# v of batch 0's first four heads in one load and product, seven dummies behind ident for twelve, w_in's last load split, batch 2's sums called one quarter ahead

## The chip, the cores and the metric

The kernel runs on one core of one Trainium2 chip. The metric is the device time of one execution in microseconds (us). Four runs of the kernel before gave 502.73, 502.10, 504.18 and 502.46 us, a median of 502.6. One more execution was profiled; its own time was 503.14 us, of which 501.4 us lie between the first and the last instruction (the span). All times of day below are counted from the start of that span.

## The reference, cut to what matters

Attention in which keys and values are first projected along the sequence (1024 rows to 64), then a feed-forward layer with a hard-swish-like gate:

```python
k_proj = np.einsum('ks,bhsd->bhkd', E, k)          # 8 batches, 8 heads, 1024 x 64 -> 64 x 64
v_proj = np.einsum('ks,bhsd->bhkd', F, v)
attn = softmax(q @ k_proj^T / sqrt(64))            # 1024 x 64 for each head
x = (attn @ v_proj), heads side by side            # 8192 tokens x 512
h = x @ w_in                                       # 512 -> 2048
out = (h * clip(h + 3, 0, 6) / 6) @ w_out          # 2048 -> 512
```

Inputs and output are float32; the kernel multiplies in bfloat16 and sums in float32.

## The kernel before, in words

The work goes batch by batch, and each batch in two blocks of 512 tokens (`t`). For a block, sixteen groups `first_group` (`fo`) make the hidden layer `g`, each of eight matmuls with the stationary half as wide as the array (L169, two of them side by side on the array), a Relu on ACT (L513) and a multiply on DVE (L514). Four groups `second_group` then multiply a block's `g` with `w_out`, each in four quarters of eight matmuls, copy the result out of PSUM and store it by SP (L549). The attention of a later batch is placed by hand between these groups: a dictionary `plan` says, for slot `n` (0 to 7 in a batch) and quarter, which piece of it is recorded there (L654 to L668). The scheduling is manual: every engine executes its instructions in the order in which the Python code records them, and the framework adds only the waits.

For batches 2 to 7 the softmax's sums are made by DVE: `add_up` (L270) reduces the exponentials of each pair of heads, `spread_sums` (L279 to L284) turns, adds and inverts them, and SP writes the result to DRAM (L287) and reads it back broadcast as `rec` (L293). The products of attention and v are multiplied with `rec` on DVE (L262). For batch 2, inside the pass over batch 1 (`b == 1`), the last of these calls, `end_of_sums`, stands at slot 5, quarter 2.

Batch 0 has no earlier work to hide behind, and has a class of its own, `First`. The opening:

- SP and ACT load E and F (L78, L79); DVE sets `ones`; TensorE runs twelve dummy matmuls on `ones` (L89). They compute nothing that is used.
- POOL issues the loads of batch 0, in an order written by hand: k and half of q by pairs of heads (L106, L102), with the identity matrix `ident` made by POOL between the first and the second pair; then four pairs of v; then w_in in eight pieces of columns (L125), the other half of q, w_out (L133) and the inputs of batch 1 (L120). A load waits for the landing of the load eight places before it.
- E and F are cast, transposed on TensorE with `ident` (L145), and copied to `e_t` and `f_t`.
- `first_block` goes over four pairs of heads: `keys` (L375, copied by DVE at L378), `queries` (transposes, L405, L409), `scores` (L418) with exponentials on ACT (L445), `keys_transposed` (L384, L386) and `sums` (L425), whose logarithm and exponential on ACT (L450, L451) give the reciprocal. A few single dummies stand in between.
- Then come, in this order: `vals(0)` (the projection of v for heads 0 and 1: eight matmuls at L391 into PSUM and a copy at L394), `sums(2)`, `vals(1)`, `products(0)` (attention times v on PE at L425, times the reciprocal on DVE at L454, into `xT`), `sums(3)`, `vals(2)`, `products(1)`, a dummy, `products(2)`, `vals(3)` with its copy on ACT, the first two matmuls of the hidden layer, and `products(3)`. After that the hidden layer of block 0 runs on.

Of the kernel before, what the change touches and what calls it, by code (L numbers as in the profile page):

```python
# [15 lines left out]
def kernel(  # L16
# [11 lines left out]
    nc = tc.nc  # L28
# [5 lines left out]
    P = 128  # L34
    SO = S // P
    KO = d_model // P
# [29 lines left out]
    def pmm():  # L66
        return ps_mm.tile([P, TOK], f32, tag="mm", name="mm")

    def pat():
        return ps_at.tile([P, TOK], f32, tag="at", name="at")  # L70


    def g_tile():
        return gpool.tile([P, FO, TOK], bf16, tag="g", name="g")
# [6 lines left out]
    ones = consts.tile([P, TOK], bf16, name="ones")  # L81
    nc.vector.memset(ones, 1.0)  # L82
    ident = consts.tile([P, P], bf16, name="ident")


    def busy(n):
        ps = pmm()
        for _ in range(n):
            nc.tensor.matmul(ps, ones[:, :P], ones, start=True, stop=True)  # L89

    busy(12)

    def raw_tile(name):
        return kqv_pool.tile([P, H, SO, D], bf16, tag=name, name=name)


    kqv = {0: {n: raw_tile(n) for n in ("k", "q", "v")}}
# [3 lines left out]
    def load_q0(t, hs):  # L101
        nc.gpsimd.dma_start(out=q0[:, t, hs], in_=kqv_dram["q"][0][:, hs, t * SB:(t + 1) * SB, :])  # L102

    def load_pair(n, j):
        hs = slice(2 * j, 2 * j + 2)
        nc.gpsimd.dma_start(out=kqv[0][n][:, hs], in_=kqv_dram[n][0][:, hs])  # L106

    for j in range(KO):
        load_pair("k", j)
        load_q0(0, slice(2 * j, 2 * j + 2))  # L110
        if j == 0:
            make_identity(nc, ident)
    for j in range(KO):
        load_pair("v", j)

    def load_kqv(b, order="qkv"):
        kqv[b] = {}
# [6 lines left out]
    def load_w_in(lo, n):  # L124
        nc.gpsimd.dma_start(out=w_in_sb[:, :, lo:lo + n], in_=w_in_v[:, :, lo:lo + n])  # L125

    for lo, n in ((0, 128), (128, 128), (256, 256), (512, 256), (768, 256),
                  (1024, 256), (1280, 256), (1536, 512)):
        load_w_in(lo, n)
    load_q0(1, slice(0, H))  # L130
    for i in range(SB):
# [6 lines left out]
    f_t = consts.tile([P, SO, 2, KP], bf16, name="f_t")  # L138
# [9 lines left out]
    for a in range(2):  # L148
        nc.scalar.copy(f_t[:, :, a, :], ef_pv[:, 1])
    ef_t = [e_t, f_t[:, :, 0, :]]  # L150
    busy(2)

    def q_transposed(b):
# [33 lines left out]
    class Attention:  # L187
# [66 lines left out]
        def sums(self, j, *allocs):  # L254
            return self.quads(lambda r, h: ones[r:r + KP, :D], j, allocs)
# [108 lines left out]
    class First:  # L364
# [20 lines left out]
                                    self.kp[:, 2 * j + a].rearrange("p a d -> p (a d)"), ident[:KP, :KP])  # L385
            nc.vector.tensor_copy(self.kT[:, 2 * j:2 * j + 2, :].rearrange("p h m -> p (h m)"), ps)  # L386

        def vals(self, j, copy):
            ps = pat()[:, :P]
            for so in range(SO):  # L390
                nc.tensor.matmul(ps, f_t[:, so].rearrange("p a m -> p (a m)"),  # L391
                                 kqv[0]["v"][:, 2 * j:2 * j + 2, so, :],
                                 start=(so == 0), stop=(so == SO - 1))
            copy(self.vp[:, 2 * j:2 * j + 2, :].rearrange("p h d -> p (h d)"), ps)  # L394

        def queries(self, t, js):

# [39 lines left out]
        def first_block(self, meanwhile):  # L437
            recs = {}

            def scores(j):  # L440
                aT = att.tile([P, 2, HT], bf16, tag="aT0", name="aT0", bufs=KO)
                tiles = [pmm() for _ in range(2)]
                self.scores(0, j, tiles, 0)
                for r in range(2):
                    nc.scalar.activation(aT[:, r], tiles[r][:, :HT], AF.Exp, scale=scale)  # L445
                self.aT[0, j] = aT

            def sums(j):
                recs[j] = opool.tile([P, TOK], f32, tag="o_sb", name="o_sb")
                nc.scalar.activation(recs[j], self.sums(0, j, pmm), AF.Ln)  # L450
                nc.scalar.activation(recs[j], recs[j], AF.Exp, scale=-1.0)  # L451

            def products(j):
                nc.vector.tensor_mul(self.xT[:, j, 0, :], self.values(0, j, pat), recs[j])  # L454

            for j in range(KO):
                self.keys(j)
                if j > 1:
                    sums(j - 2)
                self.queries(0, (j,))  # L460
                if j > 0:
                    scores(j - 1)
                else:
                    busy(1)
                self.keys_transposed(j)
                if j < 2:
                    busy(1)
            scores(KO - 1)
            self.vals(0, nc.vector.tensor_copy)
            sums(KO - 2)  # L470
            self.vals(1, nc.vector.tensor_copy)
            products(0)
            sums(KO - 1)
            self.vals(2, nc.vector.tensor_copy)
            products(1)
            busy(1)
            products(2)
            self.vals(3, nc.scalar.copy)
            meanwhile()
            products(3)  # L480
# [35 lines left out]
    def first_group(xT, t, g, fo):  # L516
        h_ps = pmm()
        h_part(h_ps, xT, t, fo, range(KO))
        h_out(h_ps, g, fo)
# [31 lines left out]
    def whole(gen):  # L551
        for _ in gen:
            pass

    def x_tile():
        return xpool.tile([P, KO, NB, TOK], bf16, tag="xT", name="xT")
# [27 lines left out]
    def meanwhile():  # L584
        early.append(TwoGroups(xT, 0, g[0]))
        early[0].part(0, (0,))
# [13 lines left out]
    second = Attention(1)  # L600
    second.xT = x_next

    def pop():
        if later:
            later.pop(0)()
# [28 lines left out]
    second = Attention(2)  # L634
    for b in range(1, B):
        if b + 1 < B:
            x_next = second.xT = x_tile()
        third = Attention(b + 2) if b + 2 < B else None


        plan = {}
        two, more = ((pmm, pmm), (pat, pat)), (pat, pat)

        def end_of_sums():
            second.add_up(3)
            second.spread_sums()

        if b == 1:
            def fourth_scores():
                while later:  # L650
                    pop()
                second.some_scores((3,), two)

            plan = {(4, 1): fourth_scores, (4, 2): lambda: second.add_up(0, 1, 2), (5, 2): end_of_sums,  # L654
                    (6, 1): second.first_values, (6, 4): second.first_products,
                    (7, 1): lambda: second.some_values((2, 3), two)}
        elif b + 1 < B:
            plan = {(5, 2): lambda: second.some_values((0, 1), two),
                    (6, 2): lambda: second.some_values((2, 3), two, third)}
            if third:  # L660
                plan[4 if b == 2 else 3, 2] = third.projected
            if b == 2:
                plan.update({(0, 2): second.projected, (1, 4): second.all_scores,
                             (2, 2): lambda: second.add_up(0, 1, 2), (3, 2): end_of_sums})
            else:
                plan.update({(0, 1): lambda: second.some_scores((1, 2, 3), (*two, more)),
                             (0, 2): lambda: second.add_up(0), (1, 2): lambda: second.add_up(1, 2),
                             (2, 2): end_of_sums})  # L668


        slots = (0, 3, 11, 15) if b == 1 else (3, 7, 11, 15)
        for t in range(NB):
            g = g_tile()
            for fo in range(FO):
                if b < 3 and t == 0 and fo < 2:

                    if fo == 0:
                        TwoGroups(xT, t, g).parts((0, 1, 2), (3,))
                else:
                    first_group(xT, t, g, fo)  # L680
                pop()
                if b == 1 and t == 0 and fo == 1:
                    second.projected()
                elif b == 1 and t == 0 and fo == 14:
                    second.some_scores((2, 0, 1), (*two, more), later.append)
                if not behind or fo not in slots:
                    continue
                n = t * SB + slots.index(fo)

                rows = second_group(*behind[0], n % SB,  # L690
                                    nc.vector.tensor_copy if second and plan.get((n, SB)) == second.all_scores else None)
                for quarter in range(1, SB + 1):
                    next(rows) if quarter < SB else whole(rows)
                    if (n, quarter) in plan:
                        plan[n, quarter]()
            behind = [(b, t, g)]
        if b == 1:
            later.append(lambda: qT_dma.update({3: q_transposed(3)}))
        second, xT = third, x_next
# [32 lines left out]
```

## Time and profile before

| | us |
|---|---|
| median of four runs (502.10 to 504.18) | 502.6 |
| the profiled execution, its own time | 503.14 |
| its span, first to last instruction | 501.4 |
| PE busy | 494.6 (99% of the span) |
| DVE busy | 285.4 (57%) |
| ACT busy | 239.6 (48%) |
| POOL busy | 38.7 (8%) |
| start of the steady stream of matmuls at L169 | 20.77 |

In the lines of the profile, PE is the matmul, PEld the weight load that overlaps it, DVE VectorE, ACT ScalarE, POOL GpSimd and SP SyncE; L12 is line 12 of the kernel; `out<-in` are the program's own names of tiles. A line of the timeline gives the start, the length, the engine, the line, the operation, how often it ran in a row (x8), and in brackets how long the engine sat idle before it and what ended that. The chain of waits is followed back from the last instruction: each piece is a start, a length and what ran. Busy shares are averages over the whole span, and a matmul's end is modelled, so PE's 99% says that it always had something in hand, not that it ran at its peak.

Loads of the opening, by the landing events of the trace (issue on POOL, landing):

| load | issue | landing |
|---|---|---|
| k, pair 0 | 1.24 | 6.23 |
| k, pair 3 | 6.16 | 12.61 |
| q half, pair 3 | 6.87 | 13.29 |
| v, pair 0 | 7.58 | 14.56 |
| v, pair 1 | 8.29 | 15.84 |
| v, pair 2 | 9.00 | 17.12 |
| v, pair 3 | 9.71 | 18.42 |
| w_in, columns 0 to 127 | 10.94 | 20.06 |
| w_in, last 512 columns | 18.70 | 29.83 |
| q, other half | 20.34 | 32.59 |

### The profile page before, as it was taken

To read this page: it belongs to the slowest core of one execution; us is meant where nothing else is said; L and a number is where in the kernel's file an instruction comes from. 1 tells how busy PE (TensorE), PEld (TensorE's weight loads), DVE (VectorE), ACT (ScalarE), POOL (GpSimd) and SP (SyncE) were. 2 spreads that over 40 slices of the span, in tenths; PEclk is the share of its full clock that TensorE was granted. 3 is DMA by queue.
4 is the path that set the end of the run, shared out by engine and by line. 5 is a ranking of instruction groups with operands and counts; after the bars stand their busy time and mean duration, and the time that the engine had idled before them with its cause. 6 is when DMAs were issued, how large, how long until landed. Compare 5 with 4: busy or idle time off the path is not lost.

```text
span 501.4 us, 11177 instructions
## 1 busy us (share of the span) xinstructions
PE 494.6 (99%) x4802; PEld 256.5 (51%) x4802; DVE 285.4 (57%) x438; ACT 239.6 (48%) x414; POOL 38.7 (8%) x58
## 2 busy tenths in 40 slices
PE   8999999999999999999999999999999999999997
PEld 4554554555555445555555555555455555555554
DVE  3572736886659665666638655674755656334420
ACT  3657566665354345533564344643456344343431
POOL 8620020200020020002000020000000000000000
PEclk9999999999999999999999999999999999999999
DMA  9999999898759699549960799309511261101112
GB/s 167 198 204 207 188 172 234 149 211 177 181 94 221 140 217 212 115 107 228 204 129 22 172 192 221 83 24 221 126 43 44 59 176 44 43 22 43 44 43 84
DMA packets 83618, 68.43 MB, mean 136 GB/s; under 512 B 38256, under 2 KB 69232, under 8 KB 83568
## 3 DMA queue, kind: packets, MB, share of 16 engines
q0 software_dynamic: 32480, 29.36, 37.5%
q1 hardware_dynamic: 50864, 38.02, 30.9%
q8 instruction: 37, 0.61, 0.5%
q10 hardware_dynamic: 224, 0.33, 0.3%
q14 instruction: 13, 0.11, 0.1%
HBM read 71.83 MB, written 16.97 MB: 177 GB/s over the span
## 4 chain that ended last, share of the span: by engine, by line
PE 94%; DMA 5%; POOL 1%; issue 0%; SPq 0%; ACT 0%; ACTq 0%; POOLq 0%
PE mm L169 87%; PE at L169 2%; DMA w_in_sb<-in_moe_w_in_dram 2%; DMA qT<-q 2%; DMA k<-in_k_dram 1%; PE mm L250 1%; PE at L229 1%; PE at L250 1%; PE mm L229 1%; PE at L425 0%; POOL q L102 0%; POOL k L106 0%; PE at L405 0%; PE at L418 0%; POOL ident masks.py:199 0%
## 5 line engine op out<-in xcount | busy, mean ns | idle before, releaser
L514 DVE SCALAR_TENSOR_TENSOR g<-r,mm 128x512 bf16<-128x512 f32 x256 | 174.3, 687 | 144.3 <-ACT r L513 143.6
L169 PE MATMUL mm<-w_out_sb,g 128*64 128x512 bf16 (+2 forms) x2080 | 235.6, 376 | 0.0
L169 PE MATMUL mm<-xT,w_in_sb 128*64 128x512 bf16 x2048 | 231.1, 379 | 0.2 <-DMA w_in_sb<-in_moe_w_in_dram 0.2
L513 ACT ACTIVATE r<-mm 128x512 f32<-128x512 f32 x256 | 152.7, 598 | 74.4 <-PE mm L169 73.4
L169 PEld LDWEIGHTS <-w_in_sb 128*64 128x64 bf16 x2048 | 115.8, 110 | 104.9 <-issue 0.6
L169 PEld LDWEIGHTS <-g 128*64 128x64 bf16 x2080 | 115.0, 110 | 106.3 <-issue 7.1
L548 ACT COPY o_sb<-mm 128x512 f32<-128x512 f32 x58 | 34.0, 586 | 149.9 <-PE mm L169 149.5
L270 DVE TRANSPOSE_TENSOR_REDUCE parts<-aT 128x32 f32<-128x1024 bf16 x24 | 28.8, 1226 | 0.0
L262 DVE TENSOR_TENSOR xT<-at,rec 128x512 bf16<-128x512 f32 x32 | 20.5, 683 | 8.7 <-ACT rec L181 5.8
L238 ACT ACTIVATE aT<-at 128x512 bf16<-128x512 f32 x38 | 20.7, 620 | 8.7 <-PE at L229 8.7
L262 DVE TENSOR_TENSOR xT<-mm,rec 128x512 bf16<-128x512 f32 x24 | 15.5, 686 | 7.3 <-PE mm L250 7.2
L219 POOL COPY mark<-qT 1x1 bf16<-1x1 bf16 x5 | 0.9, 177 | 203.0 <-DMA qT<-q 203.0
L205 DVE CAST kp<-at 64x512 bf16<-64x512 f32 x14 | 9.0, 678 | 11.3 <-PE at L169 11.2
L169 PE MATMUL at<-k,e_t 128*64 128x512 bf16 x56 | 13.2, 379 | 0.0
L169 PE MATMUL at<-v,f_t 128*64 128x512 bf16 x56 | 13.2, 379 | 0.0
L238 ACT ACTIVATE aT<-mm 128x512 bf16<-128x512 f32 x18 | 9.7, 603 | 7.1 <-PE mm L229 7.1
L208 DVE CAST vp<-at 64x512 bf16<-64x512 f32 x14 | 9.7, 694 | 0.4
L538 DVE COPY o_sb<-mm 128x384 f32<-128x384 f32 x1 | 0.6, 558 | 15.2 <-PE mm L169 15.2
L169 PEld LDWEIGHTS <-e_t 128*64 128x64 bf16 x56 | 6.2, 110 | 5.7
L89 PE MATMUL mm<-ones 128*128 128x512 bf16 x18 | 7.4, 549 | 1.5 <-DVE ones L82 1.5
L229 PEld LDWEIGHTS <-kT 64*64 64x64 bf16 x224 | 5.6, 106 | 5.6 <-issue 4.7
L229 PE MATMUL at<-qT,kT 64*64 64x256 bf16 x152 | 6.2, 269 | 0.9 <-DMA qT<-q 0.9
(68 smaller groups left out, 148.2 us busy)
## 6 DMA issues: line engine op xcount, KB each, us to landing
out_dram<-o_sb SPq DMA_DIRECT2D x63, 256.0 KB, 4.4
rec<-turned_rows SPq DMA_DIRECT2D x48, 256.0 KB, 6.3
k<-in_k_dram POOLq DMA_DIRECT2D x7, 1024.0 KB, 10.6
v<-in_v_dram POOLq DMA_DIRECT2D x7, 1024.0 KB, 16.4
q<-in_q_dram POOLq DMA_DIRECT2D x7, 1024.0 KB, 20.8
w_out_sb<-in_moe_w_out_dram POOLq DMA_DIRECT2D x4, 512.0 KB, 16.1
w_in_sb<-in_moe_w_in_dram POOLq DMA_DIRECT2D x5, 256.0 KB, 9.8
k<-in_k_dram POOLq DMA_DIRECT2D x4, 256.0 KB, 5.6
```

Of the source, the lines that this page charges most:

```text
L89: nc.tensor.matmul(ps, ones[:, :P], ones, start=True, stop=True)
L169: nc.tensor.matmul(ps[lo:lo + width], stationary[:, lo:lo + width], moving, **flags)
L205: nc.vector.tensor_copy(self.kp[:, :, a, :], self.ps[:KP].rearrange("p (h d) -> p h d", d=D))
L208: nc.vector.tensor_copy(self.vp[a * KP:(a + 1) * KP], self.ps[KP:].rearrange("p (h d) -> p h d", d=D))
L229: nc.tensor.matmul(tiles[r][t * KP:(t + 1) * KP, a * HT:(a + 1) * HT], self.kT[r * D:(r + 1) * D, 2 * j + a, :], qT[r * D:(r + 1) * D, j, ...
L238: when(lambda r=r: nc.scalar.activation(aT[:, :, r, :], tiles[r].rearrange("p (a n) -> p a n", a=2), AF.Exp, scale=scale))
L250: nc.tensor.matmul(tiles[t][c:c + D], stationary(r, 2 * j + a), self.weights(j, a)[r:r + KP], start=True, stop=True)
L262: when(lambda t=t: nc.vector.tensor_mul(self.xT[:, j, t, :], av[t], rec[:, t]))
L270: nc.vector.tensor_reduce(out=self.parts[:, j], op=ALU.add, axis=mybir.AxisListType.X, apply_transpose=True, in_=self.aT[j].rearrange("p a ...
L513: nc.scalar.activation(r, h_ps, AF.Relu, bias=0.5, scale=1.0 / 6.0)
L514: nc.vector.scalar_tensor_tensor(g[:, fo, :], r, 1.0, h_ps, op0=ALU.min, op1=ALU.mult)
L548: (copy or nc.scalar.copy)(o_sb, o_ps)
```

## The change

Five edits:

- the dummies at the start are seven instead of twelve, are recorded after `ident` has been made, and use `ident` instead of `ones` as the stationary (as do all other dummies);
- v of heads 0 to 3 of batch 0 comes in one load instead of two;
- the projection of these four heads is one product of eight matmuls with 256 columns instead of two with 128, with one copy, and `sums(2)` is recorded between its fourth and fifth matmul; `sums(3)` comes next, and `products(0)` and `products(1)` come ahead of `vals(2)`;
- the last 512 columns of w_in come in two loads instead of one;
- `end_of_sums` of batch 2 stands at quarter 1 of slot 5 instead of quarter 2.

```diff
-            nc.tensor.matmul(ps, ones[:, :P], ones, start=True, stop=True)
-
-    busy(12)
+            nc.tensor.matmul(ps, ident, ones, start=True, stop=True)
...
-    def load_pair(n, j):
-        hs = slice(2 * j, 2 * j + 2)
+    def load_pairs(n, j, more=1):
+        hs = slice(2 * j, 2 * (j + more))
         nc.gpsimd.dma_start(out=kqv[0][n][:, hs], in_=kqv_dram[n][0][:, hs])
...
         if j == 0:
             make_identity(nc, ident)
-    for j in range(KO):
-        load_pair("v", j)
+            busy(7)
+    load_pairs("v", 0, 2)
+    for j in range(2, KO):
+        load_pairs("v", j)
...
-                  (1024, 256), (1280, 256), (1536, 512)):
+                  (1024, 256), (1280, 256), (1536, 256), (1792, 256)):
...
-        def vals(self, j, copy):
-            ps = pat()[:, :P]
+        def vals(self, j, copy, more=1, halfway=lambda: None):
+            hs = slice(2 * j, 2 * (j + more))
+            ps = pat()[:, :more * P]
             for so in range(SO):
-                nc.tensor.matmul(ps, f_t[:, so].rearrange("p a m -> p (a m)"),
-                                 kqv[0]["v"][:, 2 * j:2 * j + 2, so, :],
+                nc.tensor.matmul(ps, f_t[:, so].rearrange("p a m -> p (a m)"), kqv[0]["v"][:, hs, so, :],
                                  start=(so == 0), stop=(so == SO - 1))
-            copy(self.vp[:, 2 * j:2 * j + 2, :].rearrange("p h d -> p (h d)"), ps)
+                if so == SO // 2 - 1:
+                    halfway()
+            copy(self.vp[:, hs, :].rearrange("p h d -> p (h d)"), ps)
...
             scores(KO - 1)
-            self.vals(0, nc.vector.tensor_copy)
-            sums(KO - 2)
-            self.vals(1, nc.vector.tensor_copy)
-            products(0)
+            self.vals(0, nc.vector.tensor_copy, 2, lambda: sums(KO - 2))
             sums(KO - 1)
+            products(0)
+            products(1)
             self.vals(2, nc.vector.tensor_copy)
-            products(1)
             busy(1)
             products(2)
...
-            plan = {(4, 1): fourth_scores, (4, 2): lambda: second.add_up(0, 1, 2), (5, 2): end_of_sums,
+            plan = {(4, 1): fourth_scores, (4, 2): lambda: second.add_up(0, 1, 2), (5, 1): end_of_sums,
```

More of the change, by code (lines that the diff above doesn't have):

```diff
@@ L102, in load_q0 @@
         nc.gpsimd.dma_start(out=q0[:, t, hs], in_=kqv_dram["q"][0][:, hs, t * SB:(t + 1) * SB, :])
-    def load_pair(n, j):
-        hs = slice(2 * j, 2 * j + 2)
+    def load_pairs(n, j, more=1):
+        hs = slice(2 * j, 2 * (j + more))
         nc.gpsimd.dma_start(out=kqv[0][n][:, hs], in_=kqv_dram[n][0][:, hs])
     for j in range(KO):
-        load_pair("k", j)
+        load_pairs("k", j)
         load_q0(0, slice(2 * j, 2 * j + 2))
@@ L468, in first_block @@
             scores(KO - 1)
-            self.vals(0, nc.vector.tensor_copy)
-            sums(KO - 2)
-            self.vals(1, nc.vector.tensor_copy)
+            self.vals(0, nc.vector.tensor_copy, 2, lambda: sums(KO - 2))
+            sums(KO - 1)
             products(0)
-            sums(KO - 1)
+            products(1)
             self.vals(2, nc.vector.tensor_copy)
-            products(1)
             busy(1)
```

## The prediction

> **What bounds the kernel now.** I read the page's busy times first, then the chain of work that ended last in order of time, then the timeline of the first 22 us.
>
> ```profile
> PE 494.6 (99%) x4802; PEld 256.5 (51%) x4802; DVE 285.4 (57%) x438; ACT 239.6 (48%) x414; POOL 38.7 (8%) x58
> ```
>
> TensorE is busy for 494.6 of 501.4 us, so a change pays only where the matmul stream starts earlier or loses a gap. The chain shows two such places:
>
> ```profile
> 10.94 9.12 DMA w_in_sb<-in_moe_w_in_dram
> 20.11 0.41 PE mm L169 x2
> 20.51 0.33 PE at L425 x2
> 20.84 12.85 PE mm L169 x118
> ...
> 176.03 8.01 DMA qT<-q
> 184.09 0.41 PE at L229 x8
> ```
>
> The steady stream begins at 20.77 (20.84 in the chain's rounding); from there one piece of PE follows another, but for one wait of about 1 us at 184.09, for the transposed q of batch 4. The change touches the time ahead of 20.77 and, by its words, batch 2 around 109. In the timeline of the opening the reader is to see how tightly PE, DVE and ACT hand work to each other:
>
> ```profile
> 1.46 5.30 PE L89 MATMUL mm<-ones 128*128 128x512 bf16 x12 [1.46 <-DVE ones L82]
> 5.58 0.62 ACT L141 CAST g<-g 128x512 bf16<-128x512 f32 x1 [2.95 <-DMA g<-in_E_dram]
> 6.55 0.90 PE L145 MATMUL at<-ident,g 128*128 128x128 bf16 x8
> 7.29 0.59 PE L89 MATMUL mm<-ones 128*128 128x512 bf16 x2
> ...
> 16.51 0.40 PE L425 MATMUL mm<-aT,ones 64*64 64x512 bf16 x2
> ...
> 17.50 0.29 DVE L394 CAST vp<-at 128x128 bf16<-128x128 f32 x1 [0.66 <-PE at L391]
> ...
> 17.91 0.69 DVE L454 TENSOR_TENSOR xT<-at,o_sb 128x512 bf16<-128x512 f32 x1
> ...
> 18.52 0.28 DVE L394 CAST vp<-at 128x128 bf16<-128x128 f32 x1
> ...
> 18.95 0.40 PE L425 MATMUL at<-aT,vp 64*64 64x512 bf16 x2
> ...
> 20.44 0.40 PE L425 MATMUL at<-aT,vp 64*64 64x512 bf16 x2
> ...
> 20.77 1.49 PE L169 MATMUL mm<-xT,w_in_sb 128*64 128x512 bf16 x12
> ```
>
> **Batch 2's sums: nothing.** The call moves from the second to the first quarter of one slot. Between those quarters only matmuls are recorded, on PE's queue; the call itself records only on DVE (L270, L279 to L284) and SP (L287, L293). No other DVE, ACT or SP instruction stands between the two places, so every queue keeps its order. In the trace the last reduce of batch 2 starts at 109.50, when the multiply of g before it (108.90 + 0.69) ends: it waits for DVE, not for a quarter. Cost and gain 0. The products at 121.84 still wait 1.9 us for their sums, and PE shows no gap there.
>
> **The loads: about nothing.** The load queue is full: in the stretches from 7 to 21 us the 16 DMA engines show a share of 1.27 to 1.49 (packets overlap) and move 183 to 203 GB/s. Loads land in order: the landing events put the four v pairs at 14.56, 15.84, 17.12 and 18.42, the first w_in piece at 20.06. Merging two v loads saves one issue on POOL (0.75 us) and moves no byte, so I put the double load's landing at 15.84, where the second pair lands today, and the first w_in piece at 20.06. Each load waits for the one eight places earlier, so all later ones shift by one place until the split of the last w_in restores the count; q's second half is issued about 0.7 us later (now 20.34) behind a queue that is still full. It lands at 32.59 today and is needed at 33.70. The split itself hides: the last w_in lands at 29.83, its first use is about 12 groups of 0.86 us behind 20.8. If that cover were gone, each later us of landing would cost a us. Bounds: -0.1 to +0.3; I take 0.
>
> **One product for v's first four heads: +0.93 us.** Today PE runs product, sums, product, then the first attention product (17.40), whose v projection was copied long before. After, I follow the new order with durations of the rows.
> - The product of v starts at 15.89 as now: the scores before it end then, and 15.84 + 0.05 is the landing. A pair of 512-column matmuls takes 0.218 (12.85 us for 118 in the chain), so a 256-column one is spaced 0.11, and four end their issue at 16.34. The sums wait for the exponentials until 16.51, as now. The other four run from 16.84 to 17.18, and the last result stands at 17.45.
> - DVE copies 256 columns. 128 columns take 0.29, 64x512 take 0.68 (L205), so about 0.42: 17.49 to 17.91. PE does the fourth sums at 17.38 and then has nothing: the first attention product needs this copy and starts at 17.97 (+0.06, as after e_t: 7.91 to 7.97). That is +0.57 against 17.40.
> - The second follows at 18.19, the third v product at 18.52 to 18.92 (now 17.74).
> - DVE takes its queue in order, and the copy of this third product now stands behind two multiplies of xT instead of one: 18.45, then 19.11 (spacing 0.66 as at 18.80), then the copy 19.72 to 20.00 (now 18.52 to 18.80). PE's third attention product starts at 20.06; now 18.95. This is the term that decides: +1.11.
> - The fourth v product 20.39 to 20.79, ACT's copy of it 21.05 to 21.31, the first piece of the hidden layer (now held until 20.11 by w_in, which has landed by then) 20.94, the fourth attention product 21.37; now 20.44. So +0.93: 0.18 of the delay comes back because that w_in wait vanishes.
> - The stream begins at 21.70 instead of 20.77. The fourth multiply ends at 22.6, and the matmuls that need it come at 21.70 + 5 x 0.216 = 22.78, so no further wait.
>
> What is queued behind PE's two new waits is everything, since PE's order is fixed.
>
> **Seven dummies for twelve: -0.07 to +0.9, I take +0.17.** Ident is ready at 3.35, so the dummies start near 3.45 instead of 1.46; the first is spaced 0.40, the others 0.43 (weight loads at 4.85, 5.27, 5.70), and the transposes start at 6.41 instead of 6.55; the casts they also need end at 6.20. These 0.14 us run through the keys' chain, but the double load of v (15.84) and PE's four wide matmuls give back half: -0.07. Against it stands TensorE's rate. In the trace dummies are spaced 0.43 up to 6.1 and 0.21 at 7.29 (0.59 for two, less 0.38 for one), while the granted clock reads 1.00 throughout. If full rate comes at the same time, 7.1 to 7.3, the gain of 0.07 stands. If it comes the same time after the first dummy (7.29 - 1.46 = 5.83, hence 9.28), two dummies and the first keys run at half rate: transposes to 7.27, dummies to 8.12, keys at 8.15 instead of 7.97, eight matmuls at 0.107 instead of 0.056, thus +0.6; should it last over the next queries and dummies too, +0.9. The first is nearer to the row, the others keep a share.
>
> The Trainium skill, "TensorE: Matmul & The Clock Gate", Part 1, speaks against this edit: the array runs at half clock until a free-running window of about 3.4 us was busy. The trace agrees with a halved spacing; a single execution can't show that the window runs free. By the page, as an estimate, a start at 3.45 puts full rate between 6.9 and 10.3, and the sum would be about 0.3 us higher than mine.
>
> **Sum.** 0 + 0 + 0.93 + 0.17 = +1.1 us. Against the profiled execution's own time (503.14, span 501.4 and 1.7 around it) that is 504.2; it lies 0.5 above the median shown, 502.6, so the time to expect is 503.7. That the stream passes the shift on: each later stage is paced by PE, and the wait at 184.09 follows a transpose issued behind PE's products at 175.4, so it moves along.
>
> **Rivals.**
> - *Hidden anyway.* The new waits do not open, say since the wide copy or the scores come sooner, and w_in at 20.06 still sets the start, as the chain says today. Then -0.1 to +0.3: 502.5 to 502.9. Against it: the two multiplies ahead of the copy are 1.3 us of DVE that nothing takes away.
> - *Slower than 0.3%: the clock gate.* Place: PE from 6.4 to 10 us. The late dummies put off full rate; price 0.6 to 0.9 on top of 0.93, thus 504.1 to 504.5. It decides from a full rate later than about 9.2 us.
> - *The sums do what the words say.* If batch 2's chain did move, the most it could remove is the only later wait, 1.08 us at 184.09: 502.6 + 1.1 - 1.1 = 502.6. Against it: the orders are equal, and that wait belongs to batch 4.
> - *Faster.* Only if the opening also shrinks: all waits of PE from 15.9 to 20.8 are below 0.5 us today, which with 1.08 at 184 makes some 1.5 us: 501.1.
>
> **How the numbers follow.** 0.3% is 1.5 us, about what a measurement of this kernel can tell from no change: 501.1 to 504.1. Forecast 503.7 (503.2 to 504.1): 0.50. Clock gate, 504.1 to 504.8: 0.30. Hidden or removed, 502.4 to 502.9: 0.16. Faster, 501.1 or less: 0.04. The range 502.3 to 504.9 leaves out the last case and the tails. Faster 0.04, within 0.64 (of the clock gate's share some falls below 504.1, of the forecast's little above it), slower 0.32.
>
> **What would show it.** The page after should show the third attention product near 20.1, a DVE copy of v behind two multiplies, a stream that begins near 21.7 and no wait for w_in; dummies spaced 0.43 up to some time that tells the gate; batch 2's last reduce and its wait for sums shifted like everything, and the wait at 184 still near 1 us. The prediction is wrong if the third attention product starts before 19.3, if the stream's start moves without the end, or if a gap of over 0.5 us opens elsewhere.

## The result, and the profile after

The changed kernel took 504.48 us (median of 42 runs, 503.23 to 507.85), the kernel before 503.24 us in 66 runs (501.87 to 506.14). The ratio is 1.0026, with a 95% interval of 1.0019 to 1.0034: 1.0 to 1.7 us slower, where 1.1 was forecast. The time itself, 504.48, is above the forecast 503.7 and lies in the band from 504.1 that the prediction gave to the clock gate. The forecast was reckoned from four runs of the kernel before with a median of 502.6, while over 66 runs that median is 503.24. So the number alone does not choose between the two; the parts, run one by one below, have to. The profiled execution of the changed kernel took 504.12 us with a span of 502.3, 0.98 us longer than the profiled one of before (503.14).

The opening of the changed kernel, from the timeline of PE and DVE:

```profile
3.41 3.15 PE L89 MATMUL mm<-ones,ident 128*128 128x512 bf16 x7 [3.41 <-POOL ident masks.py:199]
6.37 0.67 PE L145 MATMUL at<-ident,g 128*128 128x128 bf16 x8
6.87 0.59 PE L89 MATMUL mm<-ones,ident 128*128 128x512 bf16 x2
...
16.09 0.60 PE L392 MATMUL at<-v,f_t 128*128 128x256 bf16 x4 [0.54 <-DMA v<-in_v_dram]
16.61 0.63 PE L427 MATMUL mm<-aT,ones 64*64 64x512 bf16 x2
17.18 1.04 PE L392 MATMUL at<-v,f_t 128*128 128x256 bf16 x4
18.14 0.63 PE L427 MATMUL mm<-aT,ones 64*64 64x512 bf16 x2
18.25 0.42 DVE L396 CAST vp<-at 128x256 bf16<-128x256 f32 x1 [3.06 <-PE at L392]
18.73 0.64 PE L427 MATMUL at<-aT,vp 64*64 64x512 bf16 x4
19.48 1.29 DVE L456 TENSOR_TENSOR xT<-at,o_sb 128x512 bf16<-128x512 f32 x2 [0.80 <-PE at L427]
...
20.68 0.28 DVE L396 CAST vp<-at 128x128 bf16<-128x128 f32 x1
21.02 0.40 PE L427 MATMUL at<-aT,vp 64*64 64x512 bf16 x2 [0.54 <-DVE vp L396]
...
22.33 0.40 PE L427 MATMUL at<-aT,vp 64*64 64x512 bf16 x2
22.66 0.62 PE L169 MATMUL mm<-xT,w_in_sb 128*64 128x512 bf16 x4
```

The reader is to see the predicted order (one wide copy, two multiplies, then the third copy, and PE waiting for it at 21.02), but the stream begins at 22.66, not at 21.70. Two rows say why for the most part: the wide product at 17.18 takes 1.04 us where the same four matmuls at 16.09 take 0.60. TensorE ran at half rate from 16.64 to 20.05, by the record of the granted clock. The table by stretches shows it (length, busy time of PE, PEld, DVE, ACT and POOL with counts, granted clock, DMA share, GB/s):

```profile
13.00:16.60 3.60, 2.42 (x28) 1.46 (x26) 1.10 (x4) 3.07 (x9) 1.75 (x3) 1.00 1.24 205
16.60:20.00 3.40, 3.40 (x20) 1.52 (x20) 0.95 (x2) 2.37 (x4) 1.45 (x3) 0.51 1.52 191
```

So the opening is 22.66 - 20.77 = 1.89 us later in this execution, and yet the span only 0.98 longer. The difference lies in two later waits. (A wait of PE is given here as the distance of two starts less the usual 0.216 us; the idle time that a timeline shows in brackets is 0.16 less.) The wait for the transposed q of batch 4, 1.08 us at 184.09 before, is gone; in the chain PE goes straight on:

```profile
184.72 0.34 PE mm L250 x4
185.06 0.22 PE at L250 x4
185.28 0.22 PE at L229 x8
185.50 4.65 PE mm L169 x41
```

A new, smaller one, 0.24 us at 128.13, has appeared, behind the sums of batch 2, and the chain now runs through their round trip:

```profile
115.48 3.22 DMA turned_rows<-inv
...
120.91 5.17 DMA rec<-turned_rows
...
126.19 1.29 DVE xT L262 x2
127.48 0.60 DVE g L514
128.09 0.04 issue
128.13 1.05 PE mm L169 x8
```

1.89 - 1.08 + 0.24 gives 1.05; smaller gaps and rounding make up the rest to 0.98.

### The profile page after: what moved, and what is told of

Its sections match the earlier page's. It is cut to its first block, busy times and chain, and to the rows that moved or that the text cites. A ratio compares the mean times of both kernels' runs of the same rounds, so it can differ in the third digit from the quotient of the medians.

```text
span 502.3 us, 11150 instructions
## 1 busy us (share of the span) xinstructions
PE 493.6 (98%) x4789; PEld 255.7 (51%) x4789; DVE 285.2 (57%) x437; ACT 239.7 (48%) x414; POOL 38.7 (8%) x58
## 4 chain that ended last, share of the span: by engine, by line
PE 92%; DMA 3%; DVE 1%; POOL 1%; SPq 0%; ACT 0%; issue 0%; DVEq 0%; ACTq 0%; POOLq 0%
PE mm L169 85%; PE at L169 2%; DMA v<-in_v_dram 2%; PE mm L250 1%; DMA rec<-turned_rows 1%; PE at L229 1%; PE at L250 1%; DMA turned_rows<-inv 1%; PE mm L229 1%; POOL q L100 1%; POOL k L104 1%; PE at L392 0%; PE at L427 0%; SPq L293 0%; DVE g L514 0%
## 5 line engine op out<-in xcount | busy, mean ns | idle before, releaser
L262 DVE TENSOR_TENSOR xT<-at,rec 128x512 bf16<-128x512 f32 x32 | 20.5, 683 | 8.9 <-ACT rec L181 5.8
L89 PE MATMUL mm<-ones,ident 128*128 128x512 bf16 x13 | 5.3, 513 | 3.4 <-POOL ident masks.py:199 3.4
L503 DVE TENSOR_TENSOR xT<-at,rec 128x512 bf16<-128x512 f32 x4 | 2.5, 684 | 8.1 <-PE at L427 8.1
```

Source lines behind the costliest of these rows:

```text
L89: nc.tensor.matmul(ps, ident, ones, start=True, stop=True)
L262: when(lambda t=t: nc.vector.tensor_mul(self.xT[:, j, t, :], av[t], rec[:, t]))
```

## The experiments

All are compared with the kernel before on the same chip. For each, the **start** is where the steady stream begins (20.77 before, 22.66 after), by its profiled execution. A ratio and its interval are taken over all runs and not from the two medians, so the us that follow from it, given behind it, differ a little from the medians' difference.

**The part on v alone** (load, product and new order; dummies, w_in and batch 2 as before). Only the added lines are shown; what they replace stands in the change above.

```diff
+    load_pairs("v", 0, 2)
...
+            self.vals(0, nc.vector.tensor_copy, 2, lambda: sums(KO - 2))
+            sums(KO - 1)
             products(0)
+            products(1)
             self.vals(2, nc.vector.tensor_copy)
```

> Only the part on v: one load and one product for the first four heads, with the new order of sums and products; dummies, w_in and batch 2 as before. Theory (the new order makes PE wait for two DVE copies): the third attention product near 20 us instead of 18.95, +0.9 us against before (0.5 to 1.4). Rival (the later dummies carry the cost): 0 within 0.3 us.

Measured: 503.67 against 502.62 us, ratio 1.0017 [1.0008, 1.0025], +0.85 us [0.4, 1.25]. The timeline of PE and DVE, here at full rate:

```profile
17.51 0.42 DVE L397 CAST vp<-at 128x256 bf16<-128x256 f32 x1 [1.89 <-PE at L393]
17.99 0.41 PE L428 MATMUL at<-aT,vp 64*64 64x512 bf16 x4 [0.18 <-DVE vp L397]
...
18.51 1.29 DVE L457 TENSOR_TENSOR xT<-at,o_sb 128x512 bf16<-128x512 f32 x2 [0.57 <-PE at L428]
19.71 0.28 DVE L397 CAST vp<-at 128x128 bf16<-128x128 f32 x1
20.05 0.40 PE L428 MATMUL at<-aT,vp 64*64 64x512 bf16 x2 [0.88 <-DVE vp L397]
...
21.36 0.40 PE L428 MATMUL at<-aT,vp 64*64 64x512 bf16 x2
21.69 0.84 PE L170 MATMUL mm<-xT,w_in_sb 128*64 128x512 bf16 x6
```

The attention products stand at 17.99, 20.05 and 21.36, the start at 21.69. The new order moves the start by 0.92 us, where 0.93 was worked out, and most of the change's loss is here.

**The dummies alone.**

```diff
-    busy(12)
...
             make_identity(nc, ident)
+            busy(7)
```

> Only the dummies: seven on ident behind ident instead of twelve on ones. Theory: -0.2 to +0.3 us, since the transposes start 0.14 us sooner and full rate comes at about the same time. Rival (late dummies put off the full rate or let it lapse): +0.6 to +1.5 us, with dummies or keys spaced at half rate behind 7.3 us, or a half-rate stretch later in the opening.

Measured: 502.96 against 502.62, ratio 1.0006 [0.9997, 1.0014]. In the profiled execution full rate came late, and the start was 21.27, half a microsecond later:

```profile
3.41 3.17 PE L89 MATMUL mm<-ones,ident 128*128 128x512 bf16 x7 [3.41 <-POOL ident masks.py:199]
6.38 1.06 PE L144 MATMUL at<-ident,g 128*128 128x128 bf16 x8
7.23 1.06 PE L89 MATMUL mm<-ones,ident 128*128 128x512 bf16 x2
8.22 1.06 PE L374 MATMUL at<-k,e_t 128*64 128x128 bf16 x8
```

The two dummies and the first keys take 1.06 us each, where before they took 0.59 and 0.63: the gate case of the prediction, to its step. But in the changed kernel's profile, with dummies at the same 3.41, full rate came at 6.40, before the keys. So the cost varies from run to run, and the measured +0.3 us (-0.15 to +0.7) lies at the theory's upper bound; the interval just reaches the rival's +0.6.

**w_in's split and the call of batch 2's sums.**

```diff
-                  (1024, 256), (1280, 256), (1536, 512)):
+                  (1024, 256), (1280, 256), (1536, 256), (1792, 256)):
...
-(5, 2): end_of_sums
+(5, 1): end_of_sums
```

> Only w_in's last load in two and batch 2's last sums called one quarter ahead. Theory: no queue but POOL's changes its order, 0 within 0.3 us, the last reduce of batch 2 still right behind the multiply of g. Rival (the sums do end a quarter sooner): the wait of DVE for rec near 121 us is 0.9 us shorter and up to 1 us is gained; or the later load of q's second half holds up its transposes near 34 us: +0.3 us or more.

Measured: 502.91 against 502.62, ratio 1.0009 [1.0000, 1.0017]. The sums do not end sooner: their rows are stored 92.56 us behind the start of the stream, 92.43 before and 92.43 in the changed kernel. The loads cause no wait either: q's second half lands at 32.97 and PE has no gap near 34. The profiled execution has a gap of 0.69 at 127, which was 0 to 1.1 us in the other kernels' profiles as well. Whether some 0.4 us are real, and from what, these runs do not settle. The three parts, each measured alone, add to +1.6 us, within their intervals of the +1.3 of the whole change.

**Ten dummies more, ahead of the stream.**

```diff
     first.first_block(meanwhile)
+    busy(10)
```

> The kernel before with ten dummies of 512 columns right behind the first block, ahead of the steady stream: a delay of 10 x 0.216 = 2.16 us put there on purpose. Theory as predicted (a shift of the opening passes through to the end): +2.0 to +2.3 us. Rival (the wait near 184 us is tied to the load queue and not to PE, and takes up the shift): +0.9 to +1.4 us, and no wait of PE near 186 us in the profile.

Measured: 506.07 against 502.62, ratio 1.0065 [1.0053, 1.0077]: +3.3 us [2.7, 3.9] for 2.16, more than either theory. The profiled execution (505.37, the second lowest of six) is only 2.23 us longer than that of before: it starts 1.90 later and has waits of 1.12 at 129 and 0.30 at 186. A late start is not taken up; the rival falls.

**Twenty dummies** (`busy(20)` at the same place), to see whether the excess grows.

> The kernel before with twenty dummies of 512 columns ahead of the steady stream, 4.3 us on purpose. With ten (2.16 us) the median rose by 3.3 us. Theory (a shift passes on one to one, and what was more came from the waits near 127 and 184 us, which change from run to run): +4.0 to +5.0 us. Rival (a late stream makes the later waits longer in proportion): +6 us or more.

Measured: 507.46 against 502.94, ratio 1.0092 [1.0077, 1.0108], +4.6 us [3.9, 5.4] for 4.3. Here a delay passes on one to one within the interval. With ten dummies it did not: 2.16 lies below that interval, but the 1.1 us above it did not grow with twenty. Where they came from in the unprofiled runs stays open.

**The third product of v first**: the part on v alone, but with the old place of one line.

```diff
             products(0)
-            products(1)
             self.vals(2, nc.vector.tensor_copy)
+            products(1)
```

> The part on v alone, but the third product of v stands ahead of the second attention product again, so that on DVE its copy stands behind one multiply of xT and not two. Theory (that copy's place in DVE's queue is the deciding term): the third attention product near 19.4 us instead of 20.05, the stream near 21.1 instead of 21.7, +0.2 to +0.5 us against before, 0.5 to 0.7 less than the part on v as given. Rival (the wait of PE for the wide copy decides): the first attention product still at 17.97 and the stream near 21.6, no gain over the part on v as given.

Measured: 503.29 against 502.76, ratio 1.0018 [1.0002, 1.0033]. The times (+0.9 us [0.1, 1.7]) are too coarse for 0.5 us, the timeline of PE and DVE is not:

```profile
18.52 0.69 DVE L457 TENSOR_TENSOR xT<-at,o_sb 128x512 bf16<-128x512 f32 x1 [0.57 <-PE at L428]
...
19.13 0.28 DVE L397 CAST vp<-at 128x128 bf16<-128x128 f32 x1
19.55 0.40 PE L428 MATMUL at<-aT,vp 64*64 64x512 bf16 x2
...
21.19 1.27 PE L170 MATMUL mm<-xT,w_in_sb 128*64 128x512 bf16 x10
```

The copy stands behind one multiply, the third attention product comes at 19.55 instead of 20.05, and the stream starts at 21.19: 0.50 of the 0.92 us hang on that place in DVE's queue. The other 0.42 follow the wide copy in the rows (the first attention product starts at 18.01 behind it, 17.40 before); no run takes that copy away by itself.

**The changed kernel, with dummies in PE's waits** (four of 256 columns ahead of the double product, two and three of 512 ahead of the first and third attention products).

```diff
             ps = pat()[:, :more * P]
+            for _ in range(4 * (more - 1)):
+                nc.tensor.matmul(ps, ident, ones[:, :more * P], start=True, stop=True)
...
             sums(KO - 1)
+            busy(2)
             products(0)
...
-            busy(1)
+            busy(4)
             products(2)
```

> The changed kernel with dummies where PE waits in the stretch on v: four of 256 columns ahead of the double product, two of 512 ahead of the first attention product, three more ahead of the third. They fit into waits of 0.5, 0.4 and 0.8 us. Theory (the half-rate stretch from 16.6 to 20.0 us in the changed kernel's profile comes from PE's waits): full rate in every run's opening, so no run with a mean granted clock of 0.996 or 0.997, and a median 0 to 0.3 us under the changed kernel's (+0.9 to +1.3 against before). Rival (the half rate came with the phase of the gate alone, whatever PE does): it shows in some runs still.

Measured: 504.54 against 502.76, ratio 1.0029 [1.0012, 1.0045], no gain over the change as given. None of 12 runs has a mean granted clock below 0.998 (one half-rate stretch of 3.41 us makes 0.9966). Of the changed kernel's 42 runs 5 have, of the part on v alone 2 of 11, of the same part with the third product first 1 of 12, of the kernel before 3 of the 35 in this series and none of 29 and 15 in the others. That is too rare to say that the dummies prevent it, and the mean does not tell where in a run the half rate lay.

**Batch 2's sums really earlier**: recorded two groups of the hidden layer sooner, through the list that is emptied after each group.

```diff
+            def three_sums():
+                second.add_up(0, 1, 2)
+                later.append(end_of_sums)
...
-            plan = {(4, 1): fourth_scores, (4, 2): lambda: second.add_up(0, 1, 2), (5, 2): end_of_sums,
+            plan = {(4, 1): fourth_scores, (4, 2): three_sums,
```

> The kernel before, with the last sums of batch 2 recorded two groups of the hidden layer earlier, so that DVE's order does change. Theory (the round trip through DRAM ends when the load of batch 3's v has landed, so an earlier start helps little): the rows are stored about 1.7 us sooner, land 0 to 0.5 us sooner, time -0.3 to +0.2 us. Rival (the sums' start sets their end): the rows land 1.7 us sooner, DVE's wait for rec falls from 1.9 to about 0.3 us, and PE has no gap near 127 us; -0.3 to -0.7 us on the median, since the gap there was 0 to 1.1 us in the profiles so far.

Measured: 502.53 against 502.76, ratio 0.9994 [0.9981, 1.0008]. The rows are stored 90.70 us behind the start instead of 92.43, but land at 95.38 instead of 95.64: of 1.73 us, 0.26 arrive. The load of batch 3's v lands at 95.21 here, at 95.45 before: in both the rows land 0.2 us behind it. In packets it is the same: before, the 256 packets of the two stores start from 114.70 to 116.04, the last one 0.14 us behind the end of the load's last packet; issued 1.7 us sooner, the first one starts only at 114.15.

**Batch 3's v loaded behind the sums.** POOL reads one element of the first broadcast, then issues this load.

```diff
-                load_kqv(self.b + 1, "qkv" if self.b == 2 else "kvq")
+                load_kqv(self.b + 1, "qk" if self.b == 2 else "kvq")
...
             second.spread_sums()
+            if b == 1:
+                mark = att.tile([1, 1], f32, tag="mark_v", name="mark_v", bufs=1)
+                nc.gpsimd.tensor_copy(mark, second.recs[0][:1, 0, :1])
+                kqv[3]["v"] = raw_tile("v")
+                nc.gpsimd.dma_start(out=kqv[3]["v"], in_=kqv_dram["v"][3])
```

> The kernel before, with batch 3's v loaded only once the first broadcast of batch 2's reciprocal sums has landed. Theory (the store of the rows is held by the load): from issue to landing the rows take 1.4 to 2.5 us instead of 3.2, DVE's wait for rec falls by 1 us or more, no gap of PE near 127 us; -0.2 to -0.7 us. Rival (the store takes its 3.2 us by itself): rows land as before, no gain.

Measured: 502.17 against 502.76, ratio 0.9987 [0.9975, 1.0000]. The store takes 1.4 us from issue to landing, 3.2 before, and its packets run from 113.85 to 114.56. SP's queue, of the kernel before and then of this one:

```profile
113.20 0.81 SPq L287 DMA_DIRECT2D turned_rows<-inv  x2
116.67 5.19 SPq L293 DMA_DIRECT2D rec<-turned_rows  x8
```

```profile
113.02 0.81 SPq L287 DMA_DIRECT2D turned_rows<-inv  x2
114.98 5.19 SPq L293 DMA_DIRECT2D rec<-turned_rows  x8
```

The broadcasts, which wait for the rows, follow 1.96 us behind the first store's issue instead of 3.47. DVE's longest wait for `rec` falls from 1.9 to 1.0 us, and PE has no gap near 127 or 184.

**Both of these**, the last two diffs together.

> The kernel before with both: batch 3's v loaded behind the first broadcast of batch 2's sums, and these sums recorded two groups earlier. Theory (once the load is out of the way, the start of the sums does set their end): rows land 3 us or more sooner than before (about 92.3 us behind the stream's start instead of 95.6), DVE does not wait for rec at the first products, no gap near 127 us, -0.3 to -0.9 us. Rival (nothing more to gain than by the load's place alone): the same -0.65 us, DVE still waiting.

Measured: 501.91 against 502.94, ratio 0.9984 [0.9975, 0.9993]: -0.8 us, faster than both kernels. Rows land 92.13 us behind the start, 3.5 sooner than before, and PE has no gap above 0.12 us from the start to the end. DVE still waits 0.9 us once, for a later broadcast, and nobody waits for that.

**Batch 4's q behind batch 3's sums, too.**

```diff
-                load_kqv(self.b + 1, "qk" if self.b == 2 else "kvq")
+                load_kqv(self.b + 1, "qk" if self.b == 2 else "kv" if self.b == 3 else "kvq")
...
-            if b == 1:
+            if b < 3:
+                n = {1: "v", 2: "q"}[b]
...
+                nc.gpsimd.dma_start(out=kqv[b + 2][n], in_=kqv_dram[n][b + 2])
```

> As the kernel with both, and batch 4's q loaded behind the first broadcast of batch 3's sums, too. Theory (the store of the rows is held by the load there as well): rows land within 1.5 us of their issue instead of 2.5 to 3.5, but q now lands later and shares the engines with the broadcasts, so the wait near 184 us is 0 to 1.5 us; -0.9 to +0.5 us. Rival (the transposes of batch 4's q are bound by the rows): no wait near 184 us, -0.5 us against the kernel with both.

Measured: 510.68 against 502.94, ratio 1.0147 [1.0127, 1.0167]: 7.4 us slower, where -0.9 to +0.5 was expected. The rows do land 1.4 us after their issue, but q's load, issued at 169.08, lands at 184.41, and PE stands still for 5.9 us. TensorE came back from that at half rate, which the clock's record has from 188.16 to 194.99, 6.83 us (a row of PE's timeline, then the stretches of this kernel, same columns as above):

```profile
188.84 0.64 PE L229 MATMUL at<-qT,kT 64*64 64x256 bf16 x8 [5.93 <-DMA qT<-q]
```

```profile
183.00:188.20 5.20, 0.00 (x0) 0.10 (x1) 2.21 (x4) 0.00 (x0) 0.00 (x0) 1.00 0.57 104
188.20:195.00 6.80, 6.16 (x36) 2.54 (x37) 0.00 (x0) 1.88 (x4) 2.80 (x4) 0.50 1.04 179
```

## Why the prediction was right, point by point

- **The order around v: right, mechanism and size.** +0.93 was worked out, +0.92 stands in the timeline of the part alone, where the first, third and fourth attention products came within 0.02 us of the forecast, and +0.85 [0.4, 1.25] in its runs. So the rival that the waits stay hidden falls. One reading was off without effect: the second attention product was put at 18.19, behind the first, but ran beside it from 18.00, and the third product of v came at 18.34 instead of 18.52; what follows waits for DVE. That the copy's place in DVE's queue is "the term that decides" holds for 0.50 of it.
- **The double load's landing: right in size.** 15.86 in the part alone against 15.84. In the changed kernel's profile it landed at 16.05, since the loads ahead of it were later too (the first k at 6.95 instead of 6.23, the last half of q at 13.51 instead of 13.29), and PE waited 0.54 us.
- **Batch 2's sums: right.** The rows are stored at the same 92.43 us behind the start. The rival that they would do what the words say falls.
- **w_in's split: no wait shown**, as forecast; the runs of that part leave 0 to +0.85 us open.
- **The dummies: bounds right, 0.17 taken, +0.3 [-0.15, 0.7] measured.** Neither of the two readings was right by itself. Full rate came neither at one time nor at a fixed time after the first dummy: over 13 profiles it came 2.95 to 5.85 us after it. The granted clock of 1.00 that the prediction read ahead of 7.1 was no evidence: its record begins only with the first full rate (7.12 before). The Trainium skill, "TensorE: Matmul & The Clock Gate", Part 1, says that the window is free-running; these runs agree in that its phase differs (last section). The estimate from the page (0.3 above the sum) was no worse than mine, but full rate at 6.40 in the changed kernel is sooner than the 6.9 that it gave.
- **Half rate in the middle of the opening: not foreseen.** The gate was priced only at its first opening. In the changed kernel's profile it shut again for 16.64 to 20.05, one stretch of 3.41 us. Against the part on v alone, which ran at full rate there, the start was 0.97 us later: 0.17 because the product of v began at 16.09 instead of 15.92, and 0.80 from there to the start (6.57 us instead of 5.77), with the half rate in it. Only 5 of 42 runs have a mean clock that low, so it explains this profile, not the median.
- **"The wait at 184.09 follows a transpose issued behind PE's products at 175.4, so it moves along": wrong.** It went to 0 in the changed kernel. The transposes of q in SP's queue, before and then, with those products of PE, in the changed kernel:

```profile
176.03 7.45 SPq L157 DMA_TRANSPOSE qT<-q  x2
```

```profile
176.28 6.58 SPq L157 DMA_TRANSPOSE qT<-q  x2
177.07 0.41 PE L250 MATMUL mm<-aT,vp 64*64 64x512 bf16 x4
```

The chain named PE as SP's releaser, but in the changed kernel the transposes are issued at 176.28, before those products of PE begin. They stand in SP's queue behind the broadcasts, and these wait for the rows of batch 3, which landed 0.15 to 0.17 us behind the load of batch 4's q in both kernels (166.29 after 166.12, 167.31 after 167.16). Counted from the start of the stream, the first transpose landed 2.84 us sooner in the changed kernel: 0.87 came from the rows, some 0.8 from the broadcasts' issue (5.15 us instead of 5.97), 1.2 from the transpose's own time (6.81 instead of 8.01). So this wait hangs on SP's queue and the DMAs in it, and not on those products of PE; what shortened the last two is not shown. It was 0 to 1.08 us in the profiles, apart from the kernel with q behind the sums; the gap near 127 likewise 0 to 1.12. In the changed kernel's profile this luck hid half of the opening's loss.

So the total was right in the median by its own main step, while in the two profiles a step that failed (1.08 us gone) and one that was missing (0.97 us, 0.80 of it half rate) nearly cancel.

## What to carry to other kernels

Merging two products also merges their copies: count who waits for the wider copy, and where the next copy then stands in the in-order queue of the engine that makes it. Before crediting "ends sooner", check whether any instruction of the call's own queues is passed; if only another engine's work lies between, nothing moves. And a small store followed by a read-back can end when a large load ahead of it ends: moving that load brought the rows 1.67 us forward, starting the store 1.73 us sooner only 0.26.

## What the runs showed of the hardware

- Two stores of 32x128 float32 each (16 KB), issued beside a 1 MB load, landed just behind the load, whether they were issued 1.7 us sooner or not: by 0.15 to 0.21 us in 21 of 22 cases (batches 2 and 3 of every profile, where the load stood beside them), by 0.60 in one, with ten dummies. Without the load the first took 1.4 us. The Trainium skill, "DMA: Bandwidth & Descriptors", "Queues, rings and completion order", says that each DMA engine takes its queues in turn, packet by packet. That sharing fits the packets of both, which run side by side from 114.70 on; that the stores then end with the load is what these runs add.
- The granted clock changed on a grid: in all 13 profiles the stretches between two of its changes are whole multiples of 3.413 us (1, 2, 3, 53, 92, 141 and 144 to 147 of them). Cut into such steps, every profile had PE busy for 2.95 us or more in the step that ended with full rate, and for 2.73 or less in the steps at half rate that did not. That fits the 2.95 to 5.85 us after the first dummy. What takes full rate away is less clear: the step ahead of 16.64 in the changed kernel had 2.23 us of PE, but a step with 1.58 in the kernel with q behind the sums kept it.
- After PE had stood still for 5.9 us, TensorE ran at half rate from 188.84, when it resumed, to 194.99, at a price of about 3.0 us, half of the wait itself (an estimate: 9.09 us more behind the start than in the kernel with both, less the wait of 6.09).
- The whole span behind the start of the stream is 479.2 to 479.6 us in the 12 profiles that kept full rate there, once the gaps near 127 and 184 are taken off: what varies between these profiles is the opening and these two waits.
